# One level of Strassen's scheme for the last product of a fused attention and gated feed-forward kernel

## The chip, the cores and the metric

The kernel runs on one core of one Trainium2 chip. The metric is the device time of one execution in microseconds. Before the change, three runs took 415.08 to 415.39 us, with a median of 415.28.

## What is computed

Attention with queries averaged in pairs, over 8 batches and 8 heads of 1152 positions and 64 elements, and a feed-forward part on its 4608 rows of 512:

```
q_pool = q.reshape(B, H, S // 2, 2, D).mean(axis=3)
attn   = softmax(scale * q_pool @ k.T)
x      = (attn @ v), heads side by side          # 4608 x 512
a, b   = x @ w1, x @ w2                          # 4608 x 1024 each
out    = (a * b) @ w3 @ w_out                    # 4608 x 512, float32
```

## The kernel before, in words

Everything is one stream of work, in an order that the program writes out itself. The engines each run their own instructions strictly in that order.

**Attention.** The queries and keys of two heads are cast to f16 by GpSimd (POOL: L343, L347, L349; the values at L356), turned round, and multiplied (L431, on half the height of the TensorE array, "row" mode) into one of three score buffers `psc` of two PSUM banks each. ScalarE (ACT) takes the exponential into a ring in SBUF (L436). From the ring come the products with the values (L462, and L459 for the short tiles), in one PSUM bank `avb` with two halves in turn; VectorE (DVE) divides by the sums (L483, L497, L488). 144 such groups make the rows `x`, turned round as `xT`.

**T.** Since nothing lies between w3 and w_out, the kernel first forms T = w3 @ w_out once (`t_groups`: w3 is turned at L535, copied at L538, multiplied at L544, cast into `T16` at L547). L544 multiplies 256 columns at a time. T16 lies in SBUF as 128 partitions by 8 blocks by 512 columns.

**The feed-forward part.** The 4608 rows are nine chunks of 512 tokens (`moe_groups`). For each of eight blocks of 128 hidden elements: x @ w1 into one PSUM bank, copied out as `asb` (L595 on DVE, L593 on ACT once attention is over), x @ w2 into another (both L566), and their product written as f16 into `gT` (L599, called the gate). Then the product with T: four tiles of 128 tokens, each of eight accumulating matmuls of 512 columns (L610), scaled by 1/256 into `osb` (L620; at the end half by DVE at L616 and half by ACT at L617) and stored (L574, L578). The very last tile is done in parts of 384 and 128 columns (L628, L631, L633). Stores go out through POOL's queue, and once attention is over through SP's, two of them through ACT's.

**What sets the order.** The attention part is 108 visits of three score slices each. Between two visits' scores stand one or more groups of attention times values ("A") and some "fills": pieces of the T or feed-forward work, taken from one queue in a fixed order. A fill of size 1 is eight matmuls of 256 columns or four of 512; a tile of the product with T was of size 2. A fill writes either the single bank `mo` ("m") or one of the score buffers ("s", shown as `mot`). A planner (`_Plan`, `_visits`) chooses, before anything runs, how many fills and groups each visit gets and in which bank. It has a cost for each step (0.866 us of TensorE for a fill of size 1, 1.73 for size 2, 0.69 of DVE for an evacuation) and lets a step wait for the buffer that it needs. It knows nothing of what one fill needs of another.

A chunk's fills come free when its rows are there: chunk 0 behind group 19, chunk 6 behind group 130, chunk 7 behind group 141, chunk 8 at the very end. Behind the last visit, the remaining groups alternate with one fill each (L803); then `tail` is set, DVE does a check on the sums of the exponentials (L816 to L829), and the rest of the fills follow each other with nothing between.

## Time and profile before

| what | value |
|---|---|
| timed runs, median (lowest to highest) | 415.28 us (415.08 to 415.39) |
| profiled execution: span from the first to the last instruction | 414.1 us |
| profiled execution: own time beside the span | none is given; the timed runs are 1.0 to 1.3 us above the span |
| TensorE (PE) busy | 399.9 us |
| VectorE (DVE), ScalarE (ACT), GpSimd (POOL) busy | 205.5, 323.4, 167.6 us |
| granted TensorE clock, mean | 0.999 |
| L610 matmuls of 512 columns in `mo` (during the visits) and in `mot` (behind them) | 192 and 88 |
| start of the first matmul of L610; of the last chunk's | 100.3 us; 402.25 us |
| last instruction of the attention's exponentials, about | 349 us |

Matmuls are pipelined, so a matmul's duration (379 ns for 512 columns) is longer than its step; the chain of work that ended last counts each only once, and is what tells the cost of a group. A row of a group has its busy time and the mean duration of one instruction, then the engine's idle time before it and who ended that idle time. The windows view has, for each stretch, the length and then the busy time and the number of instructions of PE, of its weight loads (PEld), of DVE, of ACT and of POOL, the granted clock, the busy share of the DMA engines and GB/s.

### The profile page before, as it was taken

The page shows a single profiled execution, that of the slowest core. Times are in us where ns is not written, and L with a number is a line of the kernel's source. Part 1 is how long each engine was busy: PE and PEld are TensorE (multiplying, and loading weights), DVE is VectorE, ACT ScalarE, POOL GpSimd, SP SyncE. Part 2 cuts the span into 40 slices and gives each one's busy share as a digit, 9 for nine tenths or more (in the row PEclk, how much of TensorE's full clock was granted, in tenths as well). Part 3 has the DMA queues.
Part 4 walks back from the last instruction along what each step waited for, and adds up shares of the span by engine and source line. Part 5 has one row for each costly group of instructions (what it writes and reads, how often), then busy time and mean ns, then how long its engine had stood idle before and what let it go on. Part 6 is the DMA issues. An engine that isn't in the chain of part 4 may idle for free.

```text
span 414.1 us, 12744 instructions
## 1 busy us (share of the span) xinstructions
PE 399.9 (97%) x5337; PEld 246.9 (60%) x5337; DVE 205.5 (50%) x573; ACT 323.4 (78%) x353; POOL 167.6 (40%) x212
## 2 busy tenths in 40 slices
PE   3899999999999999999999999999999999999995
PEld 1477787565556655566556556655777655644442
DVE  1256665665356535554455436553556346744241
ACT  4878979898989998899999999999899986022321
POOL 4979976470655316504535155505532210010000
PEclk9999999999999999999999999999999999999999
DMA  8999999999799898959999999998975440030302
GB/s 263 210 320 289 269 286 312 348 247 265 185 238 252 221 286 278 242 70 278 273 264 280 264 252 270 292 260 163 303 207 121 85 90 15 16 114 2 101 0 108
DMA packets 90832, 86.34 MB, mean 209 GB/s; under 512 B 59664, under 2 KB 64272, under 8 KB 90768
## 3 DMA queue, kind: packets, MB, share of 16 engines
q1 hardware_dynamic: 81312, 58.80, 59.1%
q0 software_dynamic: 8880, 25.63, 21.6%
q10 hardware_dynamic: 576, 1.05, 0.8%
q8 instruction: 42, 0.69, 0.7%
q14 instruction: 22, 0.18, 0.1%
HBM read 67.11 MB, written 9.44 MB: 185 GB/s over the span
## 4 chain that ended last, share of the span: by engine, by line
PE 93%; ACT 2%; DMA 2%; DVE 1%; issue 1%; SPq 0%; POOL 0%; ACTq 0%
PE psc L431 20%; PE avb L462 17%; PE mot L566 16%; PE mo L566 15%; PE mo L610 11%; PE mot L610 5%; PE mo L544 3%; PE avb L459 3%; ACT ring L436 2%; PE ptk L371 2%; DMA kst<-in_k_dram 2%; DVE kqT L373 1%; PE mot L544 1%; PE mo L535 1%; PE mot L535 1%
## 5 line engine op out<-in xcount | busy, mean ns | idle before, releaser
L436 ACT ACTIVATE ring<-psc 128x1024 f16<-128x1024 f32 x324 | 308.3, 1025 | 33.8 <-PE psc L431 32.0
L462 PEld LDWEIGHTS <-ring 128*128 128x128 f16 x2304 | 84.4, 98 | 26.3 <-issue 7.1
L431 PE MATMUL psc<-kqT 64*128 64x512 f16 (+7 forms) x1152 | 96.2, 291 | 3.4 <-ACT ring L436 0.9
L462 PE MATMUL avb<-vaug,ring 128*128 128x65 f16 x2304 | 91.4, 193 | 0.0
L343 POOL CAST kq<-kst 128x1152 f16<-128x1152 f32 x31 | 35.7, 1150 | 74.3 <-DMA kqT<-kq 52.3
L431 PEld LDWEIGHTS <-kqT 64*128 64x128 f16 x1152 | 46.0, 95 | 31.0 <-issue 8.4
L578 POOL DMA_DIRECT2D out_dram<-osb x23 | 12.7, 551 | 101.6 <-DVE rzall L483 99.9
L610 PE MATMUL mo<-T,gT 128*128 128x512 f16 x192 | 45.6, 380 | 0.0
L566 PEld LDWEIGHTS <-w2sb 128*128 128x128 f16 x320 | 28.2, 98 | 28.3 <-issue 4.2
L566 PEld LDWEIGHTS <-w1sb 128*128 128x128 f16 x320 | 28.2, 98 | 27.7 <-issue 3.9
L610 PEld LDWEIGHTS <-gT 128*128 128x128 f16 x280 | 25.3, 98 | 32.2 <-issue 5.2
L483 DVE RECIPROCAL rzall<-avb 128x2 f32<-128x2 f32 x144 | 23.8, 165 | 37.0 <-PE avb L462 20.2
L566 PE MATMUL mot<-xT,w1sb 128*128 128x512 f16 (+2 forms) x172 | 41.1, 364 | 0.1
L620 DVE TENSOR_SCALAR osb<-mo 128x512 f32<-128x512 f32 x24 | 16.6, 692 | 48.5 <-PE mo L610 48.5
L347 POOL TENSOR_TENSOR kq<-qst 128x512 f16<-128x512 f32 x31 | 39.4, 1272 | 1.2 <-DMA qst<-in_q_dram 1.2
L566 PE MATMUL mot<-xT,w2sb 128*128 128x512 f16 (+2 forms) x156 | 38.0, 368 | 0.0
L356 POOL CAST vaug<-vst 128x1152 f16<-128x1152 f32 x32 | 36.6, 1143 | 2.6 <-DMA vst<-in_v_dram 2.5
L599 DVE TENSOR_TENSOR gT<-mot,asb 128x512 f16<-128x512 f32 x37 | 25.6, 692 | 22.0 <-PE mot L566 20.8
L599 DVE TENSOR_TENSOR gT<-mo,asb 128x512 f16<-128x512 f32 x35 | 24.2, 692 | 24.6 <-PE mo L566 24.4
L566 PE MATMUL mo<-xT,w2sb 128*128 128x512 f16 (+2 forms) x164 | 36.2, 349 | 0.0
L595 DVE COPY asb<-mo 128x512 f32<-128x512 f32 x32 | 22.1, 691 | 24.0 <-PE mo L566 23.7
L566 PE MATMUL mo<-xT,w1sb 128*128 128x512 f16 (+2 forms) x148 | 33.1, 351 | 0.0
(76 smaller groups left out, 287.4 us busy)
## 6 DMA issues: line engine op xcount, KB each, us to landing
vst<-in_v_dram SPq DMA_DIRECT2D x25, 576.0 KB, 4.9
kst<-in_k_dram SPq DMA_DIRECT2D x23, 576.0 KB, 5.9
qst<-in_q_dram SPq DMA_DIRECT2D x23, 512.0 KB, 7.2
out_dram<-osb POOLq DMA_DIRECT2D x23, 256.0 KB, 5.2
kst<-in_k_dram POOLq DMA_DIRECT2D x8, 576.0 KB, 9.8
qst<-in_q_dram POOLq DMA_DIRECT2D x8, 512.0 KB, 10.4
vst<-in_v_dram POOLq DMA_DIRECT2D x7, 576.0 KB, 7.2
w3c<-in_moe_w_dram POOLq DMA_DIRECT2D x4, 512.0 KB, 8.1
```

What stands on the lines that cost most here:

```text
L343: nc.gpsimd.tensor_copy(out=kq16[:, 0:NJ].rearrange("p c u d -> p u c d"), in_=kst.rearrange("p u (c d) -> p u c d", d=D))
L347: eng.tensor_tensor(out=kq16[:, NJ:NJ + QM].rearrange("p c u d -> p u c d"), in0=qv[:, :, :, 0], in1=qv[:, :, :, 1], op=ALU.add)
L356: nc.gpsimd.tensor_copy(out=va[:, :, :, 0:D], in_=vs.pop(p).rearrange("p u (c d) -> p u c d", d=D))
L431: nc.tensor.matmul(psc[:, u, f - s * G:f - s * G + ln], kT2[u * 64:u * 64 + 64, jt, :], qpT[u * 64:u * 64 + 64, i0:i0 + ln], start=True, s ...
L436: nc.scalar.activation(out=ring[:, :, r0:r0 + G], in_=psc, func=AF.Exp, bias=0.0, scale=SCALE)
L462: nc.tensor.matmul(avb[:, o + u * E1:o + u * E1 + E1], ring[:, u, c0:c0 + 128], va[:, u, jt, :], start=(jt == 0 and u == 0), stop=(jt == N ...
L483: nc.vector.reciprocal(out=rzall[:, i, :], in_=av[:, :, D:E1].rearrange("p u o -> p (u o)"))
L566: nc.tensor.matmul(pw[:, d0:d0 + n], wt[:, mc, ft * 128:ft * 128 + 128], xT[:, mc, a:a + n], start=(mc == 0 and d0 == 0), stop=(mc == NC - ...
L595: nc.vector.tensor_copy(out=t["a"], in_=pa)
L599: nc.vector.tensor_tensor(out=t["g"][:, ft, :], in0=pb, in1=t["a"], op=ALU.mult)
L610: nc.tensor.matmul(po, t["g"][:, ft, tt:tt + 128], T16[:, ft, :], start=(ft == 0), stop=(ft == NF - 1))
L620: nc.vector.tensor_scalar_mul(out=osb, in0=po, scalar1=1.0 / (SCL * SCL))
```

## The change

A chunk's gated values G (512 tokens by 1024) and T (1024 by 512) are each cut in four: tokens in halves of 256, hidden elements in halves of 512, columns in halves of 256. One level of Strassen's scheme, in the form with fifteen sums (Winograd's), gives the four quarters of the result from seven products of quarter by quarter instead of eight. Each product is two row tiles of four matmuls of 256 columns: eight matmuls, a fill of size 1. The fills per chunk are then sixteen of the gate and seven of products, where they were sixteen and four of size 2.

The sums on T's side (four of 128x1024 f16) are made once, behind the last fill of T, into the place that held w_out. The sums on G's side are made per chunk on DVE: S1 into a tile of its own, S2, S3 and the fourth in place over quarters that are no longer needed. The sums on the result's side are folded into the evacuations (a scaled PSUM tile plus an SBUF tile in f32), with two sums of SBUF tiles beside them, which DVE makes during the attention and POOL behind it. The order of the products is 1, 2, 5, 6, 7, 4, 3; behind product 1 comes sum 3, behind 2 sum 2, behind 5 sum 4. The lower 256 rows of a chunk are whole behind product 4, the upper behind product 3, and are stored then, 128 rows at a time. The planner is told 0.6 us more of DVE for six of the fills of a chunk. Some tiles share buffers in another way than before (w3T, asb and the parts p, q, w, z have four buffers of 2 KB together; osb has two of 4 KB instead of three of 2 KB).

```diff
-    def fill(self, n, at, scored):
+    def fill(self, n, at, more, scored):
...
             self.mo = self._dve(0.2, 0.69)
+        self.dve += more
...
+        t_sums()
+
+    HF, HM, HC = NF // 2, dm // 2, 256
+    TB = {}
+
+    def t_sums():
+        b11, b12 = T16[:, 0:HF, 0:HM], T16[:, 0:HF, HM:dm]
+        b21, b22 = T16[:, HF:NF, 0:HM], T16[:, HF:NF, HM:dm]
+        ts = msb.tile([128, 4, HF, HM], FP16, tag="wo", bufs=1, name="tsum")
+        for o, x, y in ((0, b12, b11), (1, b22, ts[:, 0]), (2, b22, b12), (3, b21, ts[:, 1])):
+            nc.vector.tensor_tensor(out=ts[:, o], in0=x, in1=y, op=ALU.subtract)
+        TB.update({1: b11, 2: b21, 3: b22, 4: ts[:, 3], 5: ts[:, 0], 6: ts[:, 1], 7: ts[:, 2]})
...
+        def left(n):
+            g = t["g"]
+            lo, hi = slice(0, HC), slice(HC, CH)
+            return {1: g[:, 0:HF, lo], 2: g[:, HF:NF, lo], 3: g[:, HF:NF, lo], 4: g[:, HF:NF, hi],
+                    5: t.get("s1"), 6: g[:, 0:HF, lo], 7: g[:, 0:HF, hi]}[n]
+
+        def sums(*which):
+            g = t["g"]
+            a11, a12 = g[:, 0:HF, 0:HC], g[:, HF:NF, 0:HC]
+            a21, a22 = g[:, 0:HF, HC:CH], g[:, HF:NF, HC:CH]
+            for n in which:
+                if n == 1:
+                    t["s1"] = msb.tile([128, HF, HC], FP16, tag="s1", bufs=1, name="s1")
+                o, x, y, op = {1: (t["s1"], a21, a22, ALU.add), 2: (a11, t["s1"], a11, ALU.subtract),
+                               3: (a21, a11, a21, ALU.subtract), 4: (a12, a12, a11, ALU.subtract)}[n]
+                nc.vector.tensor_tensor(out=o, in0=x, in1=y, op=op)
...
+        def plus(out, pt, x):
+            nc.vector.scalar_tensor_tensor(out=out, in0=pt, scalar=IS, in1=x, op0=ALU.mult, op1=ALU.add)
+
+        def add(out, x, y):
+            (nc.gpsimd if tail[0] else nc.vector).tensor_tensor(out=out, in0=x, in1=y, op=ALU.add)
...
+        def out_rows(h, u):
+            if tail[0]:
+                eng = nc.scalar if c in final and u else nc.sync
+            else:
+                eng = nc.gpsimd
+            store(eng, c * CH + h * HC + u * 128, rows(h)[:, u, :])
+
+        def done(n, pt):
+            if n == 1:
+                only(part("p"), pt)
+                sums(3)
+            elif n == 2:
+                plus(rows(0)[:, :, 0:HM], pt, t["p"])
+                sums(2)
+            elif n == 5:
+                only(part("q"), pt)
+                sums(4)
+            elif n == 6:
+                plus(t["p"], pt, t["p"])
+                add(part("w"), t["p"], t["q"])
+            elif n == 7:
+                plus(part("z"), pt, t["p"])
+                add(rows(1)[:, :, HM:dm], t["z"], t["q"])
+            elif n == 4:
+                plus(rows(1)[:, :, 0:HM], pt, t["z"])
+                for u in range(2):
+                    out_rows(1, u)
+            else:
+                for u in range(2):
+                    plus(rows(0)[:, u, HM:dm], pt[:, u, :], t["w"][:, u, :])
+                    out_rows(0, u)
+
+        def product(pt, n, tiles=(0, 1)):
+            a, b = left(n), TB[n]
+            for u in tiles:
+                for f in range(HF):
+                    nc.tensor.matmul(pt[:, u, :], a[:, f, u * 128:u * 128 + 128], b[:, f, :],
+                                     start=(f == 0), stop=(f == HF - 1))
...
                 nc.vector.tensor_tensor(out=t["g"][:, ft, :], in0=pb, in1=t["a"], op=ALU.mult)
+                if ft == NF - 1:
+                    sums(1)
...
+        order7 = (1, 2, 5, 6, 7, 4, 3)
...
-            fills += [(1, 0.0)] * (2 * NF) + [(2, 0.0)] * (CH // 128)
+            fills += [(1, 0.0, 0.0)] * (2 * NF - 1) + [(1, 0.0, 0.6)] * 6 + [(1, 0.0, 0.0)] * 2
```

(`only` scales a PSUM tile into SBUF, on DVE during the attention and on ACT behind it. The last product of the last chunk is done in two halves of 128 rows, each evacuated and stored by itself.)

## The prediction

> **What bounds the kernel now.** I read the page's busy shares, then its chain of work that ended last, then that chain by windows, then the groups by shape, and last the timeline of the end. The first two are:
>
> ```profile
> PE 399.9 (97%) x5337; PEld 246.9 (60%) x5337; DVE 205.5 (50%) x573; ACT 323.4 (78%) x353; POOL 167.6 (40%) x212
> PE 93%; ACT 2%; DMA 2%; DVE 1%; issue 1%; SPq 0%; POOL 0%; ACTq 0%
> ```
>
> Busy shares alone could mislead, but the chain says the same: 93% of the path to the end is TensorE. Matmul time taken out is therefore time saved, as long as nothing else becomes late. The chain in the window from 234 us (start, duration, what, count) shows the attention stage while a chunk's product with T is placed in it:
>
> ```profile
> 237.60 1.83 PE mo L610 x8
> 239.43 0.55 PE avb L462 x18
> 239.98 0.76 PE psc L431 x12
> 240.74 1.83 PE mo L610 x8
> ```
>
> One visit is three score slices (0.76), one group of attention times values (0.55) and one tile of the product (1.83, of which 0.10 is the change from half-height scores to full height): 3.14 us, all PE. ACT needs 2.85 us for its three exponentials in it, so it has 0.3 to spare and doesn't bind first.
>
> **What is removed.** A chunk has four tiles of eight 512-column matmuls. Behind the attention, where nothing comes between, the chain has a chunk's 32 in one piece; the line below it, from the chain at 60 us, is eight matmuls of 256 columns, each with weights of its own, which is just what one of the seven products is:
>
> ```profile
> 381.69 6.91 PE mot L610 x32
> 60.27 0.87 PE mo L544 x8
> ```
>
> So a chunk goes from 6.91 to 7 x 0.87 = 6.09: **0.82 us less**. That the weight loads (98 ns each in both shapes) are 56 instead of 32 costs nothing: they lie beside matmuls 109 ns apart, as in L544's row. Nine chunks have it. The L610 rows place them: six within the visits (100 to 336 us), chunk 6 at the end of the attention (360 to 367), chunks 7 and 8 with nothing beside them (from 381 and 402). Where attention work lies between dependent steps the six give 6 x 0.82 = **-4.9 us**. For the other three the dependencies count.
>
> **What is added on VectorE.** Per chunk: four in-place sums of 128x1024 f16, two sums of 128x512 f32 (POOL does these once the attention is over), and seven evacuations instead of four. The nearest rows:
>
> ```profile
> L538 DVE COPY w3T<-mo 128x1024 f16<-128x1024 f16 x4 | 2.8, 689 | 2.4 <-PE mo L535 2.4
> L399 DVE TENSOR_TENSOR kq<-qst 128x256 f16<-128x256 f32 x2 | 0.9, 426 | 4.8 <-DMA qst<-in_q_dram 4.8
> L620 DVE TENSOR_SCALAR osb<-mo 128x512 f32<-128x512 f32 x24 | 16.6, 692 | 48.5 <-PE mo L610 48.5
> L347 POOL TENSOR_TENSOR kq<-qst 128x512 f16<-128x512 f32 x31 | 39.4, 1272 | 1.2 <-DMA qst<-in_q_dram 1.2
> ```
>
> L620 against L399 is 256 elements more for 266 ns: 1.04 ns an element and some 160 ns fixed. L538 moves 1024 f16 in 689 ns, half of that per element. A sum of two f16 tiles has no row: 0.69 if it goes like L538, 1.23 if like L399. I take **0.69**, since its operands are f16 throughout as L538's are, and L399's inputs are f32. The f32 sum is 0.69 by the slope, an evacuation 0.69 (L620); that it now also adds an SBUF tile I hold at the same, since the gate (L599), with an SBUF operand too, has 692. On POOL a f32 sum takes L347's 1.27.
>
> Is there room? Four visits around a chunk's product:
>
> ```profile
> 234.00:247.00 13.00, 13.00 (x156) 7.21 (x151) 4.52 (x13) 11.73 (x13) 5.01 (x8) 1.00 1.08 258
> ```
>
> The third busy time is DVE's: 4.52. Four evacuations leave and seven come (3 x 0.69 = 2.1), six sums come (4.1): 10.7 in about 12.2 us (13.0 less 0.8). Back-to-back DVE instructions in the timeline start some 0.08 before the one in front has ended, which gives 1 us back. So VectorE goes from a third full to 80-90%, and stays just under the PE. Queued behind it are the normalisations of attention times values (L483, L497; wanted one group later, some 2.4 us) and the release of the single bank `mo` and of the score buffers. The planner counts 0.6 us for each sum, so it can order fills around them. I take 0.1 us a chunk, **+0.6**; bounds 0 and 1 us a chunk (0 to 6).
>
> One rule speaks against this. A sum with two SBUF inputs is a new kind of work beside POOL's casts here: no such instruction of the attention stage is in the trace, so the trace can't show what the two do to each other. The Trainium skill ("SBUF — State Buffer", "SBUF: two separate sides") says a VectorE instruction with two SBUF inputs and a GpSimd instruction that reads SBUF exclude each other for a whole instruction. That is the second rival below.
>
> The four sums of T (once, at 66 us, 4 x 0.69 = 2.8 on DVE) delay the first gates of chunk 0. The visit there has 1.83 us of fills and DVE is two thirds busy; most is caught up. **+0.3**, bounds 0 and 2.8.
>
> **The chunks behind the attention.** There products follow each other without a break, and product 6 needs sum 2, which needs the evacuation of product 2 before it on the same engine. The timeline gives the lag:
>
> ```profile
> 402.25 1.03 PE L610 MATMUL mot<-T,gT 128*128 128x512 f16 x4
> 402.52 0.69 DVE L599 TENSOR_TENSOR gT<-mot,asb 128x512 f16<-128x512 f32 x1 [1.04 <-PE mot L566]
> ```
>
> Call the first product's start 0. The last gate runs 0.27 to 0.96 on DVE, sum 1 to 1.69, sum 3 to 2.4, evacuation 2 to 3.1, sum 2 to 3.75; PE has done products 1, 2 and 5 at 2.61 and **waits until 3.8**. Then 6, 7, 4 and 3 run through to 7.28, against 6.91: chunk 7 **+0.37**, no gain at all. Chunk 6 has two attention groups between its first products; with 0.85 us of that wait it comes out at **0** (bounds -0.8 and +1).
>
> **The end.** Before, one 128-row tile was stored every 1.73 us and only the last was out late: issued 409.69, 7.44 after the zero above, 4.4 us before the span's end.
>
> ```profile
> 385.00:386.00 1.00, 1.00 (x6) 0.48 (x5) 0.43 (x1) 0.35 (x1) 0.00 (x0) 1.00 0.68 262
> 409.69 0.42 ACTq L578 DMA_DIRECT2D out_dram<-osb  x1
> ```
>
> (The first line's last columns: one store of 262 KB takes 0.68 us of all DMA engines.) Now no row of the last chunk is whole before products 4 and 3. Product 6 ends at 4.67, its evacuation at 5.6, then POOL adds twice, 1.27 each: 6.95 and 8.2. The lower rows go out at 8.3 on SP and ACT, and the upper ones, ready at 8.0, are queued behind them. That is 0.85 later, and four stores (2.7 us) instead of one are outstanding: +2.0 more, less up to 0.7 since the old last store shared the queue with the one before. **+2.5**, bounds +1.2 (POOL at half the time, stores overlapping) and +5.
>
> **Sum**: -4.9 + 0.6 + 0.3 + 0 + 0.37 + 2.5 = -1.1 on the profiled span of 414.1. The page has no time of that execution beside its span; the timed runs (median 415.28) lie 1.2 above the span, and I carry that over: **414.1 us**.
>
> **Rivals.**
> (1) More of the gain stays: attention work hides every sum, chunk 6 keeps its 0.8, and the end costs 1.2: -4.9 - 0.8 + 0.4 + 1.2 = -4.1, 411.2 us. For it: the PE chain is unbroken today, and half-size fills are easier to place. Against: DVE's 80-90%.
> (2) Slower: VectorE's sums wait for POOL's casts. POOL has four casts or adds of 0.45 to 1.28 us in the 12.5 us of chunk 0's product (timeline, 106.9 to 110.8), a third of the time. Six sums that find POOL busy every third time and wait half of 1.2 lose 1.2 us a chunk, every cast hit 4 us. DVE has 1.5 us to spare, so from there each us is PE's; at 0.6 us lost a chunk it is 3.6 instead of 0.6: 417.1 us, at 1 us 419.5. The Trainium skill's page on SBUF would give this rival. L399's 426 ns, at 4 us with POOL hardly at work, can't decide it.
> (3) The f16 sums take 1.23. DVE then has 2.1 us more a chunk, 0.7 to 1.3 over what fits (take 1.3 x 6 = 7.8 instead of 0.6), T's sums 2.2 more, and three tail chunks 1.6 more each: 428 us. The Trainium skill ("VectorE: DVE Perf Modes", "The perf-mode tier table") gives tensor_tensor on 16-bit SBUF operands two elements a cycle, one on fp32; by that it is 0.69 and the sum above holds. No tensor_tensor of before with f16 inputs is there to agree.
> (4) The change doesn't do what it says: eight 256-column matmuls with weights from gT take as long as half a tile and more. Then all nine gains (7.4) go: 421.5. L544's 0.87 is the whole argument against, and a strong one.
>
> **How the numbers follow.** Chances: forecast 0.44 (own range 412.6 to 415.8), (1) 0.18, (2) 0.26, (3) 0.08, (4) 0.04. About 0.2%, 0.8 us, is what a measurement tells from no change. Of the forecast's range 0.30 lies below 414.45, 0.12 within and 0.02 above. Faster 0.30 + 0.18 = 0.48, same 0.12, slower 0.02 + 0.26 + 0.08 + 0.04 = 0.40. The range takes in (1) and most of (2): 411.0 to 419.0, leaving (3), (4) and the far ends out.
>
> **What would show it.** Right: product rows at 0.87 per eight in the chain; a DVE row of 128x1024 f16 at 0.69; PE gaps of about 1.2 us before product 6 of chunks 7 and 8; four stores within 0.5 us of each other at the end, and the last chunk's store issue to span end longer than 4.4. Wrong: DVE in the chain between 100 and 340 us with more than 1 us (rival 2 or 3, told apart by whether the sums' durations scatter or stand at 1.23), or no PE wait before product 6, which would leave chunks 6 to 8 their 0.8 each.

## The result, and the profile after

The changed kernel takes **427.59 us** (median of 4 runs, 427.3 to 428.05) where the kernel before, on the same chip, takes 415.33 (415.08 to 415.73): **1.0272 times the time, 95% interval 1.0228 to 1.0316**. The profiled execution has a span of 426.3 us against 414.1, and a mean TensorE clock of 0.989 against 0.999. The forecast was 414.1, and its range ended at 419.0.

The busy shares and the chain of work that ended last, from the page of the changed kernel:

```profile
PE 398.5 (93%) x5545; PEld 267.2 (63%) x5545; DVE 260.6 (61%) x659; ACT 322.1 (76%) x347; POOL 175.1 (41%) x216
PE 70%; DVE 6%; ACT 3%; issue 2%; POOL 0%; POOLq 0%; DVEq 0%; ACTq 0%
```

The second line adds up to only 81% of the span, as this chain can be followed back no further than 71.28 us (the one before goes back to 0.68). Of what each covers, PE is 94% before and 87% after, and DVE 1% before and 7% after (25.2 us of 345.7). Work that was beside the path is on it now.

To see where the 12.2 us of span came from, I cut both traces at the same places: the start of visit 28, where the first product is due; the start of the last visit (107); the first evacuation of chunks 7 and 8; and the span's end.

| stretch | before, us | after, us | difference |
|---|---|---|---|
| up to visit 28 | 99.50 | 103.08 | +3.6 |
| visits 28 to 106 | 246.23 | 253.04 | +6.8 |
| visit 107 to chunk 7 | 22.85 | 18.85 | -4.0 |
| chunk 7 | 20.92 | 21.23 | +0.3 |
| chunk 8 and the end | 24.6 | 30.1 | +5.5 |

The rows exchange work with each other. By visit 28 the changed kernel has done the same 36 fills as the one before, but one attention group (0.555) less, so that like for like it is 4.1 us late there and not 3.6. To separate the middle rows I give each visit a plain price from the rows of undisturbed visits: 0.86 for its scores and the change of height, 0.555 (0.74 for the mixed ones) for a group of attention times values, 0.866 for a fill and 1.73 for a tile of the old kind. Time over that price, summed over visits 28 to 106, is **3.09 us before and 9.43 after**. This "excess" is used below.

The excess comes from one execution of each kernel, and it scatters. The changed kernel and e2, e6, e7, e8 and e10 below go through the visits in the same order with the same sums (only e10 moves one of them), and their excess is 9.43 to 10.79. So a difference of up to 1.4 between two kernels may be chance.

The products themselves are as forecast: three in one piece take 2.79 us (3 x 0.87 and one matmul's end). From the timeline of the changed kernel, PE and then DVE around product 6 of the last chunk:

```profile
408.90 1.91 PE L674 MATMUL mot<-T,gT 128*128 128x256 f16 x16
410.65 1.04 PE L674 MATMUL mot<-tsum,s 128*128 128x256 f16 x8
412.58 2.79 PE L674 MATMUL mot<-tsum,gT 128*128 128x256 f16 x24 [0.88 <-DVE gT L613]
```

```profile
411.24 0.68 DVE L627 SCALAR_TENSOR_TENSOR osb<-mot,p 128x512 f32<-128x512 f32 x1
411.84 0.68 DVE L613 TENSOR_TENSOR gT<-s,gT 128x1024 f16<-128x1024 f16 x1
```

Those lines have the first product's start (408.90), product 6's start 3.68 later and the wait in front of it, put down to sum 2 on DVE (L613), which stands behind the evacuation of product 2 (L627). The forecast was 3.8.

The f16 sums cost 0.69, not 1.23, where nothing disturbs them. The groups of the changed kernel (mean ns is the last number before the bar):

```profile
L613 DVE TENSOR_TENSOR gT<-gT 128x1024 f16<-128x1024 f16 x18 | 12.6, 698 | 0.1
L613 DVE TENSOR_TENSOR s<-gT 128x1024 f16<-128x1024 f16 x9 | 7.0, 774 | 0.3
L613 DVE TENSOR_TENSOR gT<-s,gT 128x1024 f16<-128x1024 f16 x9 | 6.1, 682 | 0.0
L630 DVE TENSOR_TENSOR w<-p,q 128x512 f32<-128x512 f32 x7 | 5.4, 774 | 0.2
```

**Place 1: the sums of T.** DVE, POOL and PE at 66 to 76 us, from the timeline of the changed kernel:

```profile
66.81 1.32 DVE L565 TENSOR_TENSOR tsum<-T 128x1024 f16<-128x1024 f16 x1
68.17 1.91 DVE L565 TENSOR_TENSOR tsum<-T,tsum 128x1024 f16<-128x1024 f16 x1
70.00 0.68 DVE L565 TENSOR_TENSOR tsum<-T 128x1024 f16<-128x1024 f16 x1
71.97 0.69 DVE L691 TENSOR_TENSOR gT<-mot,asb 128x512 f16<-128x512 f32 x1
```

```profile
66.32 1.27 POOL L348 TENSOR_TENSOR kq<-qst 128x512 f16<-128x512 f32 x1 [0.21 <-DMA qst<-in_q_dram]
67.54 0.90 POOL L350 TENSOR_TENSOR kq<-qtl 64x128 f16<-64x128 f32 x1
68.39 1.14 POOL L357 CAST vaug<-vst 128x1152 f16<-128x1152 f32 x1
```

```profile
72.72 0.61 PE L432 MATMUL psc<-kqT 64*128 64x320 f16 x4 [2.75 <-DVE gT L691]
73.26 1.89 PE L579 MATMUL mo<-xT,w1sb 128*128 128x512 f16 x4
74.94 1.44 PE L372 MATMUL ptk<-ident,kq 128*128 128x128 f16 x14
```

```profile
70.00:75.00 5.00, 2.28 (x9) 0.77 (x9) 3.07 (x8) 2.81 (x3) 2.24 (x4) 0.75 0.90 308
75.00:80.00 5.00, 4.89 (x61) 3.24 (x60) 3.15 (x9) 2.31 (x3) 3.55 (x4) 0.90 0.67 223
```

Two of the four sums run beside POOL's work and take 1.32 and 1.91 instead of 0.68, and POOL's L350 takes 0.90 instead of its usual 0.45. The gate behind them (L691) is late, PE stands still for 2.75 us, and then four matmuls take 1.89 us that otherwise take 1.03. The window lines say why (PEclk is the third number from the end): the granted clock is 0.75 and 0.90, so about 3.4 us ran at half speed.

**Place 2: the visits.** PE and DVE at the products of chunk 2:

```profile
203.25 1.03 PE L674 MATMUL mo<-tsum,gT 128*128 128x256 f16 x8
204.74 0.71 PE L463 MATMUL avb<-vaug,ring 128*128 128x65 f16 x18 [0.45 <-DVE xb L498]
```

```profile
201.66 0.94 DVE L613 TENSOR_TENSOR gT<-gT 128x1024 f16<-128x1024 f16 x1
202.52 0.68 DVE L627 SCALAR_TENSOR_TENSOR p<-mo,p 128x512 f32<-128x512 f32 x1
203.24 1.05 DVE L630 TENSOR_TENSOR w<-p,q 128x512 f32<-128x512 f32 x1
204.40 0.29 DVE L498 TENSOR_TENSOR xb<-avb,rzall 128x128 f16<-128x128 f32 x1
```

PE's attention group at 204.74 waits for a normalisation (L498) that takes 0.29, because a sum, an evacuation and another sum run ahead of it on DVE. The 13 visits with products that end on an attention group or have three fills hold 4.2 us of the excess of 9.43. In four of them (42, 43, 59 and 86, 2.5 us together) the trace puts PE's wait down to DVE; in visit 45 (0.7 us) it names an exponential of ACT.

Another 2.6 us is one of order: 13 visits put the attention group first, then a fill in the score buffer, then one in `mo` ("Asm"), and each takes 3.39 to 3.41 us where the order "msA" takes 3.14. The chain in the one that starts at 198.4:

```profile
198.48 0.34 PE psc L432 x4
...
198.91 1.03 ACT ring L437
...
199.99 1.05 PE mot L674 x8
```

Between scores and product stands an exponential of ACT: the fill waits for a score buffer that it still reads.

DVE's load in a chunk's product is what had been forecast. The window of chunk 4's (busy of PE, PEld, DVE, ...) has 9.98 us of 12.0, 83%:

```profile
281.00:293.00 12.00, 11.74 (x160) 8.34 (x157) 9.98 (x21) 10.34 (x12) 5.56 (x6) 1.00 0.94 235
```

**Place 3: the end.** GpSimd's last sums, ACT's stores, and the windows of the end (the last two numbers are the share of all DMA engines and GB/s):

```profile
414.52 1.27 POOL L630 TENSOR_TENSOR w<-p,q 128x512 f32<-128x512 f32 x1 [18.51 <-DVE p L627]
415.76 1.26 POOL L630 TENSOR_TENSOR osb<-z,q 128x512 f32<-128x512 f32 x1
```

```profile
417.05 0.99 ACTq L591 DMA_DIRECT2D out_dram<-osb  x2
```

```profile
418.00:419.00 1.00, 0.00 (x0) 0.00 (x0) 0.00 (x0) 0.00 (x0) 0.00 (x0) 1.00 1.00 373
419.00:420.00 1.00, 0.00 (x0) 0.00 (x0) 0.00 (x0) 0.00 (x0) 0.00 (x0) 1.00 1.01 375
420.00:421.00 1.00, 0.00 (x0) 0.00 (x0) 0.00 (x0) 0.00 (x0) 0.00 (x0) 0.85 0.79 283
421.00:422.00 1.00, 0.00 (x0) 0.00 (x0) 0.00 (x0) 0.00 (x0) 0.00 (x0) 0.50 0.00 0
```

The four stores are issued 8.15 us after the last chunk's first product and their data ends at 420.96, 2.5 later than before's against the same zero; 8.3 and +2.5 were forecast. But the span goes on to 426.3. In the trace's raw instructions, SP and ACT take their closing branch at 418.06, and the next instruction of either runs only at 422.76: 4.7 us. Before, ACT took 2.9 for that (410.13 to 413.07), and SP had branched at 408.07, beside the last matmuls. Only then does SP work through its list of some twenty semaphore waits, 2.6 us, which before had also lain beside other work.

This part scatters too. Six kernels have the same end (the changed one, e1, e2, e3, e5 and e9), and from the first evacuation of chunk 8 to the span's end they take 28.7 to 30.1 us; five with the plain end (before, e4, e6, e11 and e12) take 24.4 to 25.4. The changed kernel's execution is the longest of its six, so the +5.5 of the table is about 4.5 between the two means.

### The profile page after: what moved, and what is told of

Its sections match the earlier page's. It is cut to its first block, busy times and chain, and to the rows that moved or that the text cites. A ratio compares the mean times of both kernels' runs of the same rounds, so it can differ in the third digit from the quotient of the medians.

```text
span 426.3 us, 13233 instructions
## 1 busy us (share of the span) xinstructions
PE 398.5 (93%) x5545; PEld 267.2 (63%) x5545; DVE 260.6 (61%) x659; ACT 322.1 (76%) x347; POOL 175.1 (41%) x216
## 3 DMA queue, kind: packets, MB, share of 16 engines
q10 hardware_dynamic: 576, 1.05, 0.7%
## 4 chain that ended last, share of the span: by engine, by line
PE 70%; DVE 6%; ACT 3%; issue 2%; POOL 0%; POOLq 0%; DVEq 0%; ACTq 0%
PE mot L579 16%; PE psc L432 15%; PE mo L579 14%; PE avb L463 13%; PE mot L674 5%; PE mo L674 4%; ACT ring L437 3%; PE avb L460 2%; DVE gT L613 1%; DVE gT L691 1%; DVE osb L627 1%; DVE w L630 1%; DVE p L627 1%; DVE s L613 1%; DVE kqT L374 0%
## 5 line engine op out<-in xcount | busy, mean ns | idle before, releaser
L691 DVE TENSOR_TENSOR gT<-mo,asb 128x512 f16<-128x512 f32 x44 | 30.4, 692 | 39.8 <-PE mo L579 39.5
L579 PE MATMUL mot<-xT,w1sb 128*128 128x512 f16 (+1 forms) x232 | 52.4, 353 | 0.1
L674 PEld LDWEIGHTS <-gT 128*128 128x128 f16 x432 | 40.5, 97 | 10.1 <-DVE gT L613 3.1
L579 PEld LDWEIGHTS <-w2sb 128*128 128x128 f16 x320 | 27.6, 98 | 30.1 <-issue 7.0
L579 PE MATMUL mo<-xT,w2sb 128*128 128x512 f16 (+1 forms) x204 | 45.6, 352 | 0.0
L348 POOL TENSOR_TENSOR kq<-qst 128x512 f16<-128x512 f32 x31 | 40.3, 1299 | 0.7 <-DMA qst<-in_q_dram 0.7
L357 POOL CAST vaug<-vst 128x1152 f16<-128x1152 f32 x32 | 36.6, 1144 | 2.3 <-DMA vst<-in_v_dram 2.2
L685 ACT COPY asb<-mot 128x512 f32<-128x512 f32 x16 | 9.4, 585 | 36.5 <-PE mot L579 36.5
L498 DVE TENSOR_TENSOR xb<-avb,rzall 128x128 f16<-128x128 f32 x96 | 28.0, 292 | 3.4
L691 DVE TENSOR_TENSOR gT<-mot,asb 128x512 f16<-128x512 f32 x28 | 19.4, 691 | 17.3 <-PE mot L579 17.0
L687 DVE COPY asb<-mot 128x512 f32<-128x512 f32 x35 | 24.2, 692 | 7.5 <-PE mot L579 7.4
L579 PE MATMUL mot<-xT,w2sb 128*128 128x512 f16 (+1 forms) x116 | 28.8, 372 | 0.0
L579 PE MATMUL mo<-xT,w1sb 128*128 128x512 f16 (+1 forms) x88 | 22.6, 382 | 0.0
```

The source lines that it names most:

```text
L348: eng.tensor_tensor(out=kq16[:, NJ:NJ + QM].rearrange("p c u d -> p u c d"), in0=qv[:, :, :, 0], in1=qv[:, :, :, 1], op=ALU.add)
L357: nc.gpsimd.tensor_copy(out=va[:, :, :, 0:D], in_=vs.pop(p).rearrange("p u (c d) -> p u c d", d=D))
L498: nc.vector.tensor_tensor(out=xbt, in0=av[:, :, 0:D], in1=rzall[:, i, :].unsqueeze(2).to_broadcast([128, 2, D]), op=ALU.mult)
L579: nc.tensor.matmul(pw[:, d0:d0 + n], wt[:, mc, ft * 128:ft * 128 + 128], xT[:, mc, a:a + n], start=(mc == 0 and d0 == 0), stop=(mc == NC - ...
L674: nc.tensor.matmul(pt[:, u, :], a[:, f, u * 128:u * 128 + 128], b[:, f, :], start=(f == 0), stop=(f == HF - 1))
L687: nc.vector.tensor_copy(out=t["a"], in_=pa)
```

## The experiments

Two theories stood for the visits at first. **O**: the order costs, which the planner chooses because it is told of 0.6 us of DVE per product. **D**: the sums cost, by the load they put on DVE. For the rest, the sums of T and the end were each to be tested alone.

| kernel | median us | ratio to before (95%) | span | visits 28 to 106, us | excess |
|---|---|---|---|---|---|
| before | 415.3 | | 414.1 | 246.23 | 3.09 |
| changed | 427.59 | 1.0272 (1.0228 to 1.0316) | 426.3 | 253.04 | 9.43 |
| e1 | 432.08 | 1.0402 (1.0312 to 1.0492) | 426.1 | 255.54 | 12.67 |
| e2 | 426.34 | 1.0244 (1.0179 to 1.0309) | 424.1 | 253.84 | 10.22 |
| e3 | 423.84 | 1.0199 (1.0128 to 1.0269) | 421.3 | 251.01 | 7.40 |
| e4 | 416.63 | 1.0007 (0.9965 to 1.0049) | 414.0 | 246.69 | 3.51 |
| e5 | 420.25 | 1.0098 (1.0064 to 1.0133) | 422.3 | 246.66 | 3.79 |
| e6 | 421.20 | 1.0116 (1.0056 to 1.0176) | 419.1 | 254.40 | 10.79 |
| e7 | 426.17 | 1.0228 (1.0171 to 1.0285) | 424.8 | 253.70 | 10.09 |
| e8 | 424.80 | 1.0228 (1.0163 to 1.0293) | 422.6 | 253.31 | 9.69 |
| e9 | 422.74 | 1.0162 (1.0108 to 1.0216) | 420.8 | 250.55 | 6.93 |
| e10 | 424.94 | 1.0204 (1.0155 to 1.0254) | 425.7 | 253.50 | 9.88 |
| e11 | 414.65 | 0.9955 (0.9935 to 0.9976) | 413.0 | 250.22 | 6.61 |
| e12 | 413.14 | 0.9926 (0.9899 to 0.9953) | 412.0 | 249.63 | 5.15 |

e1's four runs took 427.95, 429.73, 434.44 and 434.86, so its visits say more than its median, which is over all four.

**e1: the planner is told of no sums.**

```diff
-[(1, 0.0, 0.6)] * 6
+[(1, 0.0, 0.0)] * 6
```

> The changed kernel, with one number of the planner changed: it is told 0 instead of 0.6 us of VectorE for the six fills of a chunk that carry a sum, so that it chooses another order of the same work. Theory O (order): the visits lose because the allowance makes the planner put the attention group in front of two fills (3.40 us a visit in the trace of after) where groups behind the fills cost 3.14. The plan then has about 12 such visits less, at 0.26 each: about 3 us faster than after, 424.5 us. Theory D (VectorE is the bound in the product stretches, and the allowance keeps the damage small): without it PE waits more often for buffers, and the time is the same or longer, 427.5 to 431 us.

Measured: no gain. The products now follow in the order "msA", and ten visits behind them take 3.4 to 4.3 us: in each PE waits for DVE's normalisation (L498), 6.7 us in all. The excess is 12.67 instead of 9.43. The allowance is a hedge that costs less than what it wards off, so O alone is wrong.

**e2: the sums of T one at a time**, behind gates 1, 3, 5 and 6 of chunk 0.

```diff
-        t_sums()
+                if c == 0 and ft in (1, 3, 5, 6):
+                    t_sum((1, 3, 5, 6).index(ft))
```

> The changed kernel, with the four sums of T made one at a time behind the gates 1, 3, 5 and 6 of chunk 0 instead of all at once behind the last fill of T. Theory T (the burst): four sums in a row, two of them drawn out to 1.3 and 1.9 us beside POOL's casts, hold a score buffer so long that PE stands for 2.75 us and its granted clock then falls to half for some 3 us; spread, all of it goes: 4 us less than after, 423.5 us. Rival: the sums cost the same wherever they stand, since VectorE must do them in any case; at most 1 us less, 426.5 us.

Measured: visit 28 starts at 100.70, 2.4 earlier than after the change and still 1.2 later than before; the clock stays at 1.00. So only part of this loss is the burst. Four other kernels make the four sums in one burst and keep their clock (e3, e6, e8, e9, in the table further down); their visit 28 starts at 100.53 to 101.12, about as early as here. What spreading saved is therefore the loss of clock, and not the sums themselves.

**e3: no sums in chunks 0 to 5**, in the same order of fills.

```diff
+            if bare:
+                return
...
-                    add(part("w"), t["p"], t["q"])
+                    t["w"] = t["p"]
```

> The changed kernel, in the same order and with the same matmuls and evacuations, without the four f16 sums and the two f32 sums of chunks 0 to 5 (their output is then not the product with T; the sums of T and those of chunks 6 to 8 stay). 36 sums of 0.69 us leave VectorE. Theory O: the order is unchanged, so only the few visits in which PE waits for a buffer or a sum gain, about 2 us: 425.5 us. Theory D: the 6.3 us that the visits lie above the forecast come back: 421.5 us.

Measured: span 421.3, between the two. In the visits the sums themselves cost only 2.0 us (253.04 to 251.01): visits 42, 43 and 59, 0.7 over their price each, come down to 0 to 0.1. Against the other kernels with the changed kernel's order it is up to 3.4. Part of the gain came from a place that the edit doesn't touch, as the burst of T's sums went better this time:

```profile
71.67 0.40 PE L432 MATMUL psc<-kqT 64*128 64x320 f16 x4 [1.71 <-DVE gT L699]
72.00 1.04 PE L579 MATMUL mo<-xT,w1sb 128*128 128x512 f16 x4
```

Against the changed kernel's lines at 72.72 the wait is 1.71 instead of 2.75, and the four matmuls behind it take 1.04 instead of 1.89: no loss of clock.

**e4: the kernel before with the group first** in its 24 tile visits.

```diff
+    order = ["Am" if x == "mA" else x for x in order]
```

> The kernel before, with the attention group put in front of the tile of the product, instead of behind it, in the 24 visits that have one of each; nothing else changes. Theory O: the order alone costs about 0.26 us a visit, so 24 x 0.26 = 6 us: 421.5 us. Rival: the order of two pieces of full-height work between the scores is free, and the 3.40 us of the changed kernel come from its smaller matmuls or its VectorE load: 415.3 us, or 0.5 more.

Measured: 416.63 us, ratio 1.0007 (0.9965 to 1.0049), each such visit 3.14. Having the group first costs nothing where the fill goes into `mo`. The 0.25 us of "Asm" is that of the fill in the score buffer.

**e5: no sums in chunks 0 to 5 and no allowance.**

```diff
+            if bare:
+                return
...
-[(1, 0.0, 0.6)] * 6
+[(1, 0.0, 0.0)] * 6
```

> Chunks 0 to 5 are left without their sums in f16 and f32 (so the output is not the product there), as in the run without sums, and besides the planner's 0.6 us of VectorE per product is set to 0, so that the order of visits is planned as if no sums existed. Theory P (the sums cost the visits twice: directly, and through the hedge that the planner buys with group-first visits): the time of visits 28 to 107 over the plain sum of their pieces, 9.43 us in the changed kernel and 7.40 without sums, falls to 3.1 to 4.5 us, about what the kernel before has (3.09); the span comes to 417 to 418.5 (421.3 without sums, 426.3 changed). Rival Q (seven evacuations and smaller products cost by themselves, whatever the order): the excess stays at 6 us or more, span 420 or more.

Measured: excess 3.79, within the 3.1 to 4.5 of theory P. So nearly all of the 6.3 us lost in the visits comes from the sums: 2.0 directly (e3), and 3.6 (7.40 to 3.79) through the order that the planner takes to make room for them. The split depends on the order: in the one that is planned without the allowance the same sums cost 8.9 (e1's 12.67 against e5's 3.79). That the products have seven evacuations and smaller matmuls costs at most 0.7. The span, 422.3, missed its expectation: T's sums took 5.97 us in this execution, PE stood still for 4.1, and the clock was 0.78 and 0.54 for 10 us.

**e6: chunks 6 to 8 plain**, with the code of the kernel before.

```diff
+        if c >= PLAIN:
+            tts = list(range(0, CH, 128))
...
+            return
         order7 = (1, 2, 5, 6, 7, 4, 3)
```

> Chunks 6, 7 and 8 are computed with the eight full products and the stores of the kernel before; chunks 0 to 5 and the sums of T stay as changed. Theory (the loss has three places that do not act on each other: T sums 3.6 to 4.4 us, visits about 6, the end 5.5 and chunk 7 0.3): from the last chunk's first product on as in the kernel before, so that the span falls by 5.0 to 6.5 from 426.3, to 420 to 421.3, with last stores out as in the kernel before. Rival (the end is late because of what goes before it, and a plain tail behind the new visits is late as well): less than 3 us, span over 423.

Measured: from the start of visit 107 to the span's end 64.2 us instead of 70.2. Of these 6.0 us, 4.65 lie behind the start of chunk 8 (25.43 against 30.08). From visit 107 to chunk 7 it is 17.22 against 18.85, but e6 does one attention group (0.55) behind the start of chunk 7 that the changed kernel does ahead of it; like for like 1.1 us are chunk 6's and 0.3 chunk 7's. In the changed kernel DVE is busy for 4.8 of each 5 us from 365 to 375, where chunk 6 has its products (the third busy time):

```profile
365.00:370.00 5.00, 4.63 (x81) 3.81 (x75) 4.84 (x14) 0.00 (x0) 0.00 (x0) 1.00 0.14 30
```

The span fell by 7.2, more than expected, as the clock did not drop at T's sums this time.

**e7: the last chunk's stores all from ACT**, so that SP is free.

```diff
-eng = nc.scalar if c in final and u else nc.sync
+eng = nc.scalar if c == max(final) or c in final and u else nc.sync
```

> All four stores of the last chunk are issued by ScalarE, so that SyncE's last store is one of chunk 7 and SyncE can take its branch some 20 us before the end. Theory S (the end is late by SyncE's late branch and its chain of waits, 4.65 and 2.6 us in the profile, behind the stores): span falls by 2 to 3.5 us, to 422.8 to 424.3. Rival X (the four stores, 1 MB that begins 8 us after the last matmuls of the last-but-one product, and the branch of the engine that issues them, set it alone): within 0.7 us of 426.3, as ScalarE's own branch comes as late as before.

Measured: span 424.8, and 28.3 instead of 30.1 us from chunk 8 on: 1.8 less, a little under what S expected and over what X allowed. Against all six kernels with the changed kernel's end (28.7 to 30.1) it is 0.4 to 1.8 less, so the direction fits S and the size is not shown. In the trace SP's list now lies beside ACT's branch (3.5 us here), and the span ends 1.9 us behind that branch's return instead of 3.5.

**e8: quarters of the last chunk stored as they are ready.**

```diff
+                for u in range(2 * last()):
+                    quarter(0, u, 0, nc.sync)
...
+                    quarter(0, u, 1, nc.scalar)
```

> In the last chunk each quarter of the output (256 rows by 256 columns) is stored when its product is done: after products 2, 7, 4 and 3, instead of all after products 4 and 3; the last two are issued by ScalarE, and SyncE is done one product earlier. Theory X (the end waits for the 1 MB of stores and for the branch fetched behind them): the data of the last quarters is 256 KB in place of 1 MB, the branch comes back in 3 us, and from the last chunk's first product to the span's end it takes 12 to 13.5 us in place of 17.4, span 421.9 to 423.4. If only SyncE's place in the queue mattered (theory S), the gain equals that of the run with the last stores on ScalarE. Rival (twice as many stores of half the row length are slower): less than 1.5 us gained.

Measured: from the first product to the end 15.4 instead of 17.4: a gain, but half of what was expected; the other five kernels with the changed kernel's end take 16.0 to 17.2. SP stood behind POOL's second sum (its end at 415.33), issued until 417.1 and branched only then. The gain is about e7's (15.6), so no gain of the shorter data at the very end is shown.

**e9: the f32 sums on GpSimd in the visits too**, and no allowance for them.

```diff
-(nc.gpsimd if tail[0] else nc.vector).tensor_tensor(...)
+nc.gpsimd.tensor_tensor(...)
-[(1, 0.0, 0.6)] * 6 + [(1, 0.0, 0.0)] * 2
+[(1, 0.0, 0.6)] * 4 + [(1, 0.0, 0.0)] * 4
```

> The two f32 sums of each chunk (w and the right half of the lower rows) run on GpSimd in the visits as well, not on VectorE, and the planner's allowance of 0.6 us stays only at the four units with an f16 sum. Theory P (VectorE's sums cost the visits, directly and through the hedge): a third of the load goes (1.4 of 4.1 us per chunk), so that a quarter to a third of the 6.3 us over the plain pieces comes back: visits 28 to 107 at 250.5 to 251.5 us in place of 253.0, excess 7.3 to 8. Rival L (GpSimd's sums hold up VectorE's instructions, as its casts held up the sums of T): excess stays at 9 or more, and VectorE's f16 rows of 0.69 show maxima over 1 us more often than in the changed kernel (3 of 24). How the burst of T sums falls this time moves the span by 0 to 4.5 us besides, so the verdict is on the visits, not on the span.

Measured: visits 250.55 us, excess 6.93, for theory P and a little better than it. GpSimd's sums take 1.27 and DVE's f16 sums show means of 680 to 783 ns, about as in the changed kernel (682 to 774): rival L is wrong here.

**e10: sum 2 ahead of the evacuation of product 2, quarters with SP clear of GpSimd** (stored as in e8, but those that wait for GpSimd's second sum come last).

```diff
-                sums(3)
+                sums(3, 2)
```

> Two edits from product 1 of chunk 7 on: the second f16 sum is made right behind the third, ahead of the evacuation of product 2 (all chunks), and in the last chunk quarters are stored as they are ready, with the one that GpSimd adds issued last, so that SyncE does not wait for GpSimd before its other stores. From the last chunk's first product to the span's end: 17.4 us in the changed kernel, about 15.5 with quarters alone (SyncE then branched at 417.16, as it stood behind GpSimd's add). Theory (product 6 waits 1.04 us for a sum that stands behind an evacuation; stores late because of GpSimd's add and because SyncE issues late): PE's gap before product 6 under 0.2 us in chunks 7 and 8, first product to last matmul 6.3 us in place of 7.3, end 12.5 to 14 us after the first product. Rival (the moved sum only makes another wait, for product 5's or 6's evacuation): the gap goes to product 7 or 4, first product to last matmul 7 us or more.

Measured: between the theories. PE's gap before product 6 is 0.48 instead of 0.88, and first product to last matmul 6.94 instead of 7.34; the gap does not go to zero because sums 1, 3 and 2 follow each other on DVE without a break, 2.2 us behind the last gate. From the first product to the end it is 15.3, no better than e8: second stores of a queue took 1.3 and 1.7 us to issue, the branches came at 419.74 and cost 3.5 to 3.6.

**e11 and e12: the cures joined.** Chunks 6 to 8 plain (e6), f32 sums on GpSimd (e9), T's four sums on GpSimd behind the sixth gate of chunk 0; e12 also moves sums 3 and 4 of each chunk there, with no allowance for them.

```diff
-            nc.vector.tensor_tensor(out=ts[:, o], in0=x, in1=y, op=ALU.subtract)
+            nc.gpsimd.tensor_tensor(out=ts[:, o], in0=x, in1=y, op=ALU.subtract)
...
+                if c == 0 and ft == 5:
+                    t_sums()
```

and, for e12 alone:

```diff
-                nc.vector.tensor_tensor(out=o, in0=x, in1=y, op=op)
+                (nc.gpsimd if n > 2 else nc.vector).tensor_tensor(out=o, in0=x, in1=y, op=op)
```

> The cures joined: chunks 0 to 5 with seven products, their f32 sums on GpSimd, the four sums of T on GpSimd behind the sixth gate of chunk 0 (a stretch in which GpSimd is idle from 92 to 110 us), chunks 6 to 8 plain as in the kernel before. If the losses are where they were found and add up: burst of T sums 1 to 4 us to nothing, visits as with the f32 sums on GpSimd (250.5 us for visits 28 to 107), chunk 6 1.6 us and the end 5.5 us back as with the plain tail; start of chunk 7 at 367 to 368 us (368.6 before, 369.8 with the f32 sums on GpSimd alone), span 412.5 to 415, ratio 0.996 to 1.003. Rival (GpSimd's sums of T, some 2.5 us each, keep VectorE's port and delay the gates, or come late for product 5): visit 28 starts over 100.8 us as before the cure, span 415.5 to 418.

> As the other kernel of this call, and of the four f16 sums per chunk two (for product 7 and for product 3) run on GpSimd as well. Theory P (VectorE's load is what the visits pay for): another 1.4 us per chunk goes from VectorE, visits 28 to 107 at 248.5 to 249.8 us, span 1 to 2 us under the other kernel's, ratio 0.99 to 1.0. Rival L (GpSimd's f16 sums take 2.5 us or more, and VectorE waits for them or beside them): visits no shorter than in the other kernel, span equal or longer, with VectorE's rows of 0.69 us showing means over 0.8.

Measured: **both are faster than the kernel before**, by 0.45% and 0.74%, with intervals clear of 1. The kernel before had 18 runs from 415.18 to 418.61 beside them; lowest against lowest, the gain is 0.27% and 0.59%. Visit 28 starts at 98.84 and 99.50 (99.50 before, with one attention group more done by then), the clock stays at 1.00, and chunk 8 begins at 387.8 and 387.0 (389.5 before). So the losses were where they were found. They came back only in part: the excess is still 6.61 and 5.15, against 3.09 before. GpSimd's groups in e12:

```profile
L613 POOL TENSOR_TENSOR gT<-gT 128x1024 f16<-128x1024 f16 x12 | 25.5, 2122 | 56.5 <-DVE s L613 26.5 <-DVE rzall L484 18.3 <-DMA qtl<-in_q_dram 10.5
L565 POOL TENSOR_TENSOR tsum<-T,tsum 128x1024 f16<-128x1024 f16 x2 | 4.2, 2120 | 0.1
L613 DVE TENSOR_TENSOR s<-gT 128x1024 f16<-128x1024 f16 x6 | 4.2, 692 | 0.2
```

A f16 sum takes three times as long there (2.12 against 0.69), but GpSimd was 41% busy in the changed kernel and is 53% busy here, no wait of PE for these sums shows in the trace, and DVE's own sums stay at 0.69 and 0.72. The chain between 100 and 340 us, by line, shows the difference; first after the change, then e12:

```profile
by line: PE psc L432 22.2%; PE mo L579 19.1%; PE avb L463 19.1%; PE mot L579 12.7%; PE mo L674 7.9%; PE mot L674 5.3%; ACT ring L437 4.6%; PE avb L460 2.9%; issue 1.7%; DVE gT L613 0.9%; DVE w L630 0.8%; DVE q L636 0.6%; DVE p L627 0.5%; DV
```

```profile
by line: PE psc L432 24.9%; PE avb L463 21.8%; PE mo L579 19.3%; PE mot L579 13.3%; PE mo L674 11.1%; PE mot L674 4.8%; PE avb L460 3.2%; ACT ring L437 0.8%; issue 0.4%; PE avb L508 0.3%; PE avb L505 0.2%; ACTq L437 0.0%
```

After the change DVE's lines and ACT's exponentials (the waits of "Asm") are in it; in e12 DVE is gone and ACT down from 4.6% to 0.8%. More than 1 us of DVE in this chain is what the prediction had named as a sign of being wrong; the four of its lines that are printed in full are 2.8% of 240 us, 6.7 us.

## Why the prediction was wrong, step by step

| term of the sum | forecast, us | measured, us | from |
|---|---|---|---|
| six chunks in the visits | -4.9 | -5.2 | six fills of 0.87 fewer |
| VectorE's stalls in the visits | +0.6 (0 to 6) | +6.3 | excess 3.09 to 9.43 (up to 10.79 in the same order); 0.7 left in e5 |
| sums of T | +0.3 (0 to 2.8) | +4.1 | start of visit 28, 3.6 later with an attention group of 0.55 less |
| chunk 6 | 0 (-0.8 to +1) | +1.1 | e6, like for like |
| chunk 7 | +0.37 | +0.3 | first evacuations |
| the end | +2.5 (1.2 to 5) | +5.5 | chunk 8 to span's end; about 4.5 between the means of six and of five executions |
| sum | -1.1 | +12.1 (span: +12.2) | |

**What was right.** A product takes 0.87. The f16 sum takes 0.69, so rival 3 was wrong. (The Trainium skill, "VectorE: DVE Perf Modes", "The perf-mode tier table", gives it two elements a cycle on 16-bit operands in SBUF; these rows agree.) PE waits before product 6, until 3.68 instead of 3.8. Chunk 7 gains nothing. The stores are issued 8.15 after the zero (8.3), and their data ends 2.5 later than before (+2.5). Rival 4, no saving on PE, was wrong.

**The step that failed most: "VectorE goes from a third full to 80-90%, and stays just under the PE. [...] The planner counts 0.6 us for each sum, so it can order fills around them."** The load came out as computed (83 to 88% in the products of three chunks), but staying under the PE on average isn't enough, as DVE runs in order and sums stand ahead of short instructions that PE waits for. And the planner's counting, booked as a help at no price, has one: it makes room by orders that cost up to 0.26 us a visit ("Asm"). e3 and e5 measure the two: 2.0 direct (up to 3.4 against the other kernels of that order) and about 3.6 in excess through the order. It was still worth its price, since without it the sums cost 8.9 (e1 against e5). My upper bound, 1 us a chunk, is about what happened; the 0.1 that I took came from an average.

**Rival 2 was right in its mechanism and wrong in size.** The sums beside POOL's work do last longer: L630's mean is 774 where 691 is undisturbed, single ones reach 1.05 (203.24) and 1.4. The five that take over 0.72 all lie beside an instruction of POOL. Over all 50 sums of the chunks on DVE that is about 2 us of DVE, a third to a half of the rival's 3.6 to 6 us. Where it struck hardest was a place that the rival didn't name, the sums of T.

**The sums of T: "delay the first gates of chunk 0 [...] most is caught up".** The four took 4.59 instead of 2.8, and PE's wait then cost the clock. Nine kernels have the same burst, with other luck in what POOL does beside it:

| kernel | four sums, us | PE stands still, us | clock 70 to 75, 75 to 80 us | visit 28 starts |
|---|---|---|---|---|
| e9 | 2.99 | 1.1 | 1.00, 1.00 | 100.78 |
| e8 | 3.19 | 1.3 | 1.00, 1.00 | 101.12 |
| e1 | 3.50 | 1.6 | 1.00, 1.00 | 99.15 |
| e3 | 3.55 | 1.7 | 1.00, 1.00 | 100.53 |
| e6 | 4.06 | 2.2 | 1.00, 1.00 | 100.56 |
| changed | 4.59 | 2.75 | 0.75, 0.90 | 103.08 |
| e7 | 4.63 | 2.8 | 0.90, 0.76 | 102.75 |
| e10 | 4.76 | 2.9 | 0.67, 0.65 | 103.92 |
| e5 | 5.97 | 4.1 | 0.78, 0.54 | 104.48 |

Like for like (an attention group of 0.55 less by then than before; in e1 and e5 instead two fills of 0.87 less) the sums cost 1.4 to 2.2 us with the clock kept, inside my bounds. With the clock lost they cost 3.8 to 5.0, and 6.7 in e5. So the clock fell where PE stood still for 2.75 us or more, and not up to 2.2; that is seen over these executions, and no experiment set the gap by hand.

The length of the wait is not the whole of it. In the traces' own record the granted clock changes only at whole steps of 3.41 us (low for 3.41 in the changed kernel and e7, for 6.83 in e5 and e10). In the step ahead of each of these falls PE stood still for 1.86 to 2.58 us in all, while from the first full clock on every step that was followed by the full clock had at most 1.68; the wait of 2.2 in e6 lay across two steps. The Trainium skill ("TensorE: Matmul & The Clock Gate", "HAM oscillation — how this bites in real kernels") warns of idle gaps over some 3.4 us; here 2.75 was enough, so the measurement decides for the shorter one. The Trainium skill's rule on the shared port ("SBUF — State Buffer", "Who interferes with whom") has the second of two such instructions wait for the first; the sums of 1.32 and 1.91 beside L348, L350 and L357 agree with it.

**Chunk 6 (0, measured +1.1)** I had set at 0 because attention groups lie between its products. Those groups load DVE too, so it is DVE that is full there (4.8 of 5 us), and PE waits.

**The end: "+2.5, bounds +1.2 [...] and +5".** The stores were forecast well; what was missing stands behind them. The closing branch of the engines that store waited 4.7 us behind 1 MB of stores (3.5 to 4.8 in the other five executions with this end, 2.9 before), and SP's list of waits moved from beside the work to behind it; e7 takes that second part away, with a gain of 0.4 to 1.8. The Trainium skill ("Runtime: NRT & Kernel Launch", "Instruction fetch mechanics") says that a taken branch out of the fetched window needs a DMA before the engine can go on; a branch that returns in 2.9 to 4.8 us, longest when the DMA engines are full, agrees with it. So do the packets of the trace's instruction queue: in the changed kernel three of 8 KB start at 420.88 to 420.96, just as the stores' data ends (420.96), and the branches return at 422.76; before, two start at 411.55 and 411.64, the data ends at 411.83 and ACT goes on at 413.07. Which engine a packet belongs to is not in the record. What remains open: e8 and e10 store less at the very end and still need 15.3 to 15.4 us from the first product to the span's end, against 11.85 before; how much of that is issue on the queues and how much the branch was not separated, and no version of the seven products with an end as short as the plain one was found.

## What to carry to other kernels

When a change takes work from the bounding engine and gives a multiple of it to an idler one, price the idler engine's queue and not its busy share: ask what short instruction, wanted soon, will stand behind the new long ones, and price every hedge that a planner takes against them at what it does to the bounding engine. Work that isn't urgent belongs on the engine that nobody waits for, even at three times the duration: that, together with leaving the tail as it was and a smaller allowance in the plan, turned 2.7% slower into 0.7% faster. And at the end of a program count what comes behind the last store, and which engine is still issuing it.

## What the runs showed that I had not expected

- One wait of PE of 2.75 us cost more than itself: 3.4 us at half clock behind it (four 512-column matmuls 1.89 us instead of 1.03), while waits of up to 2.2 us cost no clock.
- The closing branch of an engine that stores takes 2.9 us with the DMA engines half busy and 3.5 to 4.8 behind 1 MB of stores; where SP stores last, its list of waits needs another 1.4 to 2.7 behind that.
- POOL and DVE delay each other both ways: L350 0.90 instead of 0.45 beside a sum of 1.32 or 1.91 instead of 0.68; yet 12 sums of 2.12 on POOL, away from DVE's burst, left DVE's sums at 0.69 and 0.72.
